# Exp instructions with bias, scale and alpha written as immediates in a four-layer attention kernel

## The chip, the cores and the metric

The kernel runs on one core of one Trainium2 chip. The metric is the device time of one execution in microseconds (us).

Engines in the profile: PE multiplies matrices, PEld loads its weights, ACT is the scalar engine that does the exp, DVE is the vector engine. An ACTIVATE is an instruction of ACT: a function of scale x input + bias. PSUM is the memory that this kernel's matmuls write, SBUF the one where its other tiles are. An operand of an instruction is an immediate when its value stands in the instruction, and a pointer operand when it is read from a tile in SBUF.

## The reference

A 2048x512 activation passes through four layers, each with a layer norm and a residual. Layers 1 and 3 are local dilated attention (window 8). Layers 2 and 4 are full attention with 32 query heads and one shared key and value head of width 16. Those two, cut to what matters:

```python
q = (x @ wq).reshape(B, S, H, Dh).transpose(0, 2, 1, 3)      # S 2048, H 32, Dh 16
k = x @ wk
v = x @ wv
scores = einsum("bhqd,bkd->bhqk", q, k) * Dh ** -0.5
p = softmax(scores)
o = einsum("bhqk,bkd->bhqd", p, v)
return o.transpose(0, 2, 1, 3).reshape(B, S, H * Dh) @ wo
```

Each of the two layers needs 32 x 2048 x 2048 exps.

## The kernel before

A check on the norms of q and k selects a branch that needs no running maximum. There the work is cut into tiles of three chunks, each 128 keys by 512 queries of one head. Per tile: three scores matmuls into PSUM (`st`), one exp over 128x1536 from PSUM to SBUF (`pt`), and three matmuls with the values (`o_ps`). A "block" is 64 chunks. At its end the accumulator is copied and normalized, and four output-projection matmuls (`y`) are queued.

```python
def emit_exp(i):
    cs = chunks[i * tile_chunks:(i + 1) * tile_chunks]
    pt = ptp.tile([128, tile_chunks, 512], BF16, name="pt")
    pt_tiles[i] = pt
    nc.scalar.activation(out=pt[:, :len(cs), :], in_=st_tiles[i][:, :len(cs), :], func=AF.Exp, scale=scale)
    del st_tiles[i]
# ... (emit_scores, finish_block, emit_pv are cut)
for i in range(min(st_bufs, ntiles)):      # st_bufs = 2
    emit_scores(i)
for i in range(ntiles):                    # 683 tiles in each full-attention layer
    cur[0] = i
    emit_exp(i)
    if i + st_bufs < ntiles:
        emit_scores(i + st_bufs)
    emit_pv(i)
    if i % op_every == op_every - 1:       # op_every = 3
        emit_outproj(1, now=i)
```

The argument needs two more instructions, because the kernel carries its own yardstick. Both read a 128x512 fp32 tile from PSUM on ACT. The first has no pointer operand; the second takes its scale from a [128,1] tile:

```python
nc.scalar.activation(out=L[:, w, :], in_=lg[:], func=AF.Identity, scale=scale)                 # line 214
nc.scalar.activation(out=KAB[:, 0, cs], in_=ps[:], func=AF.Identity, scale=kmask[:, 0:1])      # line 354
```

Of the kernel before, what the change touches and what calls it, by code (L numbers as in the profile page):

```python
# [7 lines left out]
F32 = mybir.dt.float32  # L8
AF = mybir.ActivationFunctionType
# [460 lines left out]
def attn_B_fast(ctx, tc, QT, KAB, VE, wo_pad, x_sb, S, tag, tile_chunks=3, st_bufs=2, op_every=3, op_delay=7,  # L470
                on_qc_done=None):
    nc = tc.nc
    NT = S // 128
    NQC = S // 512
    scale = DH ** -0.5
# [16 lines left out]
    st_tiles = {}  # L492
# [14 lines left out]
    def emit_exp(i):  # L507
        cs = chunks[i * tile_chunks:(i + 1) * tile_chunks]
        pt = ptp.tile([128, tile_chunks, 512], BF16, name="pt")
        pt_tiles[i] = pt  # L510
        nc.scalar.activation(out=pt[:, :len(cs), :], in_=st_tiles[i][:, :len(cs), :], func=AF.Exp, scale=scale)  # L511
        del st_tiles[i]

    def emit_outproj(n, now=None):
# [39 lines left out]
    for i in range(ntiles):  # L554
# [5 lines that stand above are left out]
        if i % op_every == op_every - 1:  # L560
            emit_outproj(1, now=i)
# [189 lines left out]
```

## Time and profile before

| | before |
|---|---|
| time, median of the first 3 runs | 2389.79 us (2388.62 to 2390.17) |
| exp, 1366 instructions | 1860.7 us busy, 63.9 us idle before them |
| exp that follows idle, 1536 elements | 1451 ns |
| end to end of back-to-back exps | 1343 ns |
| Identity at 512 elements: no pointer / one pointer | 597 / 687 ns (medians after idle) |

The page: busy time and share of each engine; the chain of waits by line (line 511 is the exp); then the costliest groups: line, engine, operation, output and inputs, count, busy us, mean ns of one, idle us before it and what ended that idle time.

```profile
PE 2085.2 (87%) x11652; PEld 611.5 (26%) x11652; DVE 839.2 (35%) x1061; ACT 2015.7 (84%) x1603; POOL 35.7 (1%) x67
...
ACT pt L511 38%; PE st L503 11%; PE o_ps L547 8%; PE y L520 6%; DVE lb L536 3%; PE ps L184 3%; DVE prod L209 2%; PE y L265 1%; PE ps L359 1%; DVE pv L253 1%; PE acc L256 1%; DVE ot L528 1%; DVE lb L535 1%; DVE onb L537 1%; DVE qsq L373 0%
...
L503 PE MATMUL st<-QT,KAB 32*128 32x512 bf16 x4096 | 859.4, 597 | 176.1 <-ACT pt L511 168.2
L547 PE MATMUL o_ps<-pt,VE 128*32 128x512 bf16 x4096 | 864.7, 607 | 1.4 <-ACT pt L511 1.0
...
L520 PE MATMUL y<-wo_pad,onb 128*128 128x512 bf16 x256 | 155.3, 607 | 20.6 <-DVE onb L537 12.3
```

PE and ACT have similar shares, so the page's first line does not say which of them leads. The window from 300 to 1100 us lies inside the first full-attention layer. This view gives for each engine the busy us (and the instructions), then the granted PE clock:

```profile
core 0: us, PE busy (x) PEld busy (x) DVE busy (x) ACT busy (x) POOL busy (x), PEclk, DMA share, GB/s
300.00:1100.00 800.00, 727.52 (x3535) 174.40 (x3532) 226.03 (x265) 778.64 (x572) 0.00 (x0) 0.50 0.00 1
```

ACT is busy 97% of it (778.64 of 800), PE 91%, at half the clock. The ACT timeline shows the rhythm: start us, length us of the merged run, number of exps at the end of the line, and the idle time before.

```profile
472.74 8.27 ACT L511 ACTIVATE pt<-st 128x1536 bf16<-128x1536 f32 x6 [0.52 <-PE st L503]
481.19 1.45 ACT L511 ACTIVATE pt<-st 128x1536 bf16<-128x1536 f32 x1 [0.18 <-PE st L503]
482.81 25.81 ACT L511 ACTIVATE pt<-st 128x1536 bf16<-128x1536 f32 x19 [0.17 <-PE st L503]
```

Long runs of exps without a gap are tiles in which ACT leads. Lone exps with 0.18 us of idle in front (481.19, then 482.81) are 1.62 us apart: there PE leads, because the four `y` matmuls of a block come in four tiles in a row. The chain of waits shows it in such tiles elsewhere in the layer, with start us, length us and work:

```profile
805.81 0.54 PE y L520
806.35 0.54 PE st L503 x3
806.89 0.54 PE o_ps L547 x3
807.44 0.54 PE y L520
807.98 0.54 PE st L503 x3
808.52 0.55 PE o_ps L547 x3
```

A tile with `y` is three pieces of 0.54 us, 1.63 us in all, which is over the 1.343 us of an exp. Without `y` it would be about 1.08 us (an estimate from the same pieces). The 0.52 us in front of the first run belongs to the end of a block.

From the records, over both layers, I took the 1364 distances from one exp's end to the next. Their median is 1344 ns (1343 within the runs without idle); 144 lie between 1580 and 1680 ns, and 43 are over 1900 ns. In sum they exceed the median by 75 us: 41 us of it in the first set, 29 us in the second.

Groups on ACT with their shapes kept apart:

```profile
L511 ACT ACTIVATE pt<-st 128x1536 bf16<-128x1536 f32 x1364 | 1858.8, 1509 | 63.9 <-PE st L503 62.0
...
L214 ACT ACTIVATE L<-lg 128x512 f32<-128x512 f32 x16 | 9.6, 598 | 70.7 <-PE lg L212 70.7
...
L354 ACT ACTIVATE KAB<-ps,kmask 128x512 bf16<-128x512 f32 x8 | 5.5, 685 | 16.0 <-PE ps L353 16.0
```

Two readings. An operand in a [128,1] tile appears among the inputs (`kmask` on line 354); the exp lists only `st`. And the mean of 1509 ns is not the cost of an exp: back-to-back exps overlap, so a record starts while the one in front still runs. What the span pays is the distance, 1343 ns.

### The profile page before, as it was taken

How to read it: one execution, taken by the hardware profiler on the slowest of the kernel's cores; microseconds unless marked ns; L12 is line 12 of the kernel's file. 1: busy time of each engine (PE TensorE's matmuls, PEld its weight loads, DVE VectorE, ACT ScalarE, POOL GpSimd, SP SyncE). 2: the span in 40 equal slices, each digit the busy share in tenths (PEclk: the TensorE clock that was granted, in tenths of full speed). 3: DMA queues.
4: the chain of work that ended last, by engine and by line, in shares of the span. 5: the costliest groups of instructions: out<-in, count | busy, mean ns of one | idle time of the engine just before them, and what ended most of it. 6: DMA issues, size and time to landing. Idle time of an engine off the chain costs nothing.

```text
span 2389.7 us, 27720 instructions
## 1 busy us (share of the span) xinstructions
PE 2085.2 (87%) x11652; PEld 611.5 (26%) x11652; DVE 839.2 (35%) x1061; ACT 2015.7 (84%) x1603; POOL 35.7 (1%) x67
## 2 busy tenths in 40 slices
PE   5887899999999999999877879999999989999996
PEld 5433222222222222222153332222222222222221
DVE  3875222232223222322339832222222222222222
ACT  5314999999999999999842169999999999999996
POOL 1002000000000000000010000000000000000000
PEclk9998555555555555555589975555555555555555
DMA  1101000000000000000000000000000000000000
GB/s 63 37 2 28 1 1 1 1 1 1 1 1 1 1 1 1 1 1 1 1 3 2 1 1 1 1 1 9 1 1 1 1 10 1 1 9 1 1 1 11
DMA packets 14315, 11.56 MB, mean 5 GB/s; under 512 B 7904, under 2 KB 13536, under 8 KB 14048
## 3 DMA queue, kind: packets, MB, share of 16 engines
q1 hardware_dynamic: 13120, 8.60, 1.4%
q8 instruction: 95, 1.56, 0.3%
q10 hardware_dynamic: 1056, 1.05, 0.1%
q14 instruction: 44, 0.36, 0.1%
HBM read 7.37 MB, written 2.10 MB: 4 GB/s over the span
## 4 chain that ended last, share of the span: by engine, by line
ACT 39%; PE 31%; issue 17%; DVE 12%; POOL 0%; DMA 0%; ACTq 0%; SPq 0%; DVEq 0%; POOLq 0%
ACT pt L511 38%; PE st L503 11%; PE o_ps L547 8%; PE y L520 6%; DVE lb L536 3%; PE ps L184 3%; DVE prod L209 2%; PE y L265 1%; PE ps L359 1%; DVE pv L253 1%; PE acc L256 1%; DVE ot L528 1%; DVE lb L535 1%; DVE onb L537 1%; DVE qsq L373 0%
## 5 line engine op out<-in xcount | busy, mean ns | idle before, releaser
L511 ACT ACTIVATE pt<-st 128x1536 bf16<-128x1536 f32 (+1 forms) x1366 | 1860.7, 1508 | 63.9 <-PE st L503 62.0
L503 PE MATMUL st<-QT,KAB 32*128 32x512 bf16 x4096 | 859.4, 597 | 176.1 <-ACT pt L511 168.2
L547 PE MATMUL o_ps<-pt,VE 128*32 128x512 bf16 x4096 | 864.7, 607 | 1.4 <-ACT pt L511 1.0
L528 DVE COPY ot<-o_ps 128x512 f32<-128x512 f32 x64 | 44.3, 692 | 1163.2 <-PE o_ps L547 1163.2
L503 PEld LDWEIGHTS <-KAB 32*128 32x128 bf16 x4096 | 236.5, 99 | 766.1 <-issue 764.0
L547 PEld LDWEIGHTS <-VE 128*32 128x32 bf16 x4096 | 154.4, 101 | 621.4 <-issue 621.3
L521 DVE TENSOR_TENSOR x_sb<-x_sb,y 128x512 f32<-128x512 f32 x256 | 176.1, 688 | 226.1 <-PE y L520 226.1
L536 DVE RECIPROCAL lb<-lb 128x512 f32<-128x512 f32 (+1 forms) x70 | 214.9, 3075 | 2.1
L520 PE MATMUL y<-wo_pad,onb 128*128 128x512 bf16 x256 | 155.3, 607 | 20.6 <-DVE onb L537 12.3
L89 ACT ACTIVATE xn<-x_sb,ln_nmr,ln_rstd 128x512 bf16<-128x512 f32 x44 | 33.3, 806 | 92.0 <-DVE ln_nmr L83 88.8
L209 DVE TENSOR_TENSOR prod<-Qch,Kch 128x4096 bf16<-128x4096 bf16 x32 | 72.4, 2279 | 58.1 <-ACT Kch L188 56.7
L184 PE MATMUL ps<-xnT,w_sb 128*32 128x512 bf16 x1536 | 90.7, 392 | 1.9 <-ACT Vch L188 1.9
L184 PEld LDWEIGHTS <-w_sb 128*32 128x32 bf16 x1536 | 80.1, 141 | 12.1 <-issue 7.5
L256 PE MATMUL acc<-pv,ident 128*128 128x512 bf16 x256 | 68.7, 402 | 15.9 <-DVE pv L253 10.3
L212 PE MATMUL lg<-prod,ident 128*128 128x512 bf16 x256 | 60.6, 379 | 18.8 <-DVE prod L209 18.8
L258 ACT CAST Och<-acc 128x2048 bf16<-128x2048 f32 x8 | 14.9, 1866 | 72.2 <-PE acc L256 72.2
L253 DVE TENSOR_TENSOR pv<-attn,Vch 128x2048 bf16<-128x2048 bf16 x64 | 73.2, 1222 | 1.5 <-PE acc L256 1.5
L214 ACT ACTIVATE L<-lg 128x512 f32<-128x512 f32 x16 | 9.6, 598 | 70.7 <-PE lg L212 70.7
L99 PE MATMUL pT<-ident,xn 128*128 128x128 bf16 x256 | 27.6, 256 | 44.6 <-ACT xn L89 29.8
L520 PEld LDWEIGHTS <-onb 128*128 128x128 bf16 x256 | 26.4, 103 | 131.6 <-issue 89.7
L535 DVE STREAM_SHUFFLE lb<-ot 128x512 f32<-128x512 f32 (+1 forms) x70 | 46.8, 673 | 0.0
L537 DVE TENSOR_TENSOR onb<-ot,lb 128x512 bf16<-128x512 f32 (+1 forms) x70 | 44.6, 641 | 2.1
(89 smaller groups left out, 538.8 us busy)
## 6 DMA issues: line engine op xcount, KB each, us to landing
xi<-in_A_x_dram SPq DMA_DIRECT2D x4, 512.0 KB, 5.6
wo_r_73<-in_A_wo_dram SPq DMA_DIRECT2D x4, 512.0 KB, 8.2
w_sb<-in_A_wqkv_dram SPq DMA_DIRECT2D x4, 384.0 KB, 8.2
out_dram<-xo SPq DMA_DIRECT2D x2, 512.0 KB, 3.0
out_dram<-xo ACTq DMA_DIRECT2D x2, 512.0 KB, 4.9
wq_sb<-in_B_wq_dram SPq DMA_DIRECT2D x4, 128.0 KB, 3.2
woB_sb<-in_B_wo_dram SPq DMA_DIRECT2D x4, 128.0 KB, 3.7
wo_pad<-in_B_wo_dram SPq DMA_DIRECT2D x16, 32.0 KB, 1.8
```

The costliest lines, as they stand in the source:

```text
L184: nc.tensor.matmul(ps[32 * c:32 * c + 32, :], lhsT=wqkvP[:, kt, j, d, :], rhs=xnT[:, kt, c * 512:(c + 1) * 512], start=(kt == 0), stop=(kt ...
L209: nc.vector.tensor_tensor(out=prod[:], in0=Q[:, dsl, :], in1=K[:, dsl, PAD - DIL * w:PAD - DIL * w + 512], op=ALU.mult)
L253: nc.vector.tensor_tensor(out=pv[:], in0=attn[:, w, :].unsqueeze(1).to_broadcast([PCH, DG, 512]), in1=V[:, ds_, PAD - DIL * w:PAD - DIL * ...
L256: nc.tensor.matmul(acc[:, i, :], lhsT=ident[:PCH, :PCH], rhs=pv[:, i, :], start=(w == 0), stop=(w == W - 1))
L503: nc.tensor.matmul(st[:, n, :], lhsT=KAB[32 * g:32 * g + 32, a, kt * 128:(kt + 1) * 128], rhs=QT[32 * g:32 * g + 32, t, qc * 512:(qc + 1) ...
L511: nc.scalar.activation(out=pt[:, :len(cs), :], in_=st_tiles[i][:, :len(cs), :], func=AF.Exp, scale=scale)
L520: nc.tensor.matmul(y[:], lhsT=onb[:, cols], rhs=wo_pad[:, t, a, :], start=True, stop=True)
L521: nc.vector.tensor_tensor(out=x_sb[:, qt, :], in0=x_sb[:, qt, :], in1=y[:], op=ALU.add)
L535: nc.vector.stream_shuffle(out=lb[:, sl], in_=ot[:, sl], mask=[16] * 32)
L536: nc.vector.reciprocal(out=lb[:, sl], in_=lb[:, sl])
L537: nc.vector.tensor_tensor(out=onb[:, sl], in0=ot[:, sl], in1=lb[:, sl], op=ALU.mult)
L547: nc.tensor.matmul(o_ps[(qc, t, a)][32 * g:32 * g + 32, :], lhsT=VE[:, kt, :], rhs=pt[:, n, :], start=(kt == 0), stop=(kt == NT - 1), tile ...
```

## The change

The intent: an ACTIVATE that takes its bias from a [128,1] tile costs more than one with an immediate. If the default bias of the call were lowered to a pointer to a constant tile, building the instruction by hand with three immediates would take that cost off all 1366 exps.

```diff
-        nc.scalar.activation(out=pt[:, :len(cs), :], in_=st_tiles[i][:, :len(cs), :], func=AF.Exp, scale=scale)
+        ain = nc.scalar.lower_ap(st_tiles[i][:, :len(cs), :])
+        aout = nc.scalar.lower_ap(pt[:, :len(cs), :])
+        imm = lambda v: mybir.ImmediateValue(dtype=F32, value=v)
+        nc.scalar.add_instruction(mybir.InstActivation(name=nc.get_next_instruction_name(), func=AF.Exp,
+            ins=[ain, imm(0.0), imm(scale), imm(0.0)], outs=[aout]))
```

## The prediction

> **What bounds the kernel.** The page gives ACT 84% and PE 87% of the 2389.7 us span. The chain of waits gives 38% to the exp (line 511) and 17% to "issue" (mostly the part of an exp that overlaps its neighbour). The exp group is 1366 instructions, 1860.7 us busy plus 63.9 us idle before them: about 80% of the span. By windows, in 400 to 1150 us ACT is busy 97% and PE about 91%, at a granted clock of 0.50. In order of time, exps of 128x1536 that follow one another without idle end 1343 ns apart. Where ACT leads, the scores matmuls wait for it (168 us over 886 waits). After each block of 64 chunks come several tiles where the output projection makes PE the slower: there exps end 1627 ns apart and wait 0.18 us each.
>
> So 90 ns less per exp, if it shortened the distance, would be worth up to 90 ns x 1366 = 123 us (an estimate), less the PE-paced tiles.
>
> **What the change removes.** By its words, a [128,1] bias pointer on 1366 exps. I do not think it is there. Three signs:
>
> 1. Durations. The Trainium skill, "ScalarE: Activation LUTs", section "What ACT_TABLE_LOAD costs", says each [128,1] pointer operand adds about 93 ns to an ACTIVATE with immediate scale and bias, plus 0.833 ns an element. The trace has the same scale: the logits evacuation (line 214; Identity, scale and bias without a pointer, PSUM, 128x512) takes 597 ns, median; the key copies (line 354; scale from a pointer, same size) 687 ns, so 90 ns for a pointer. An exp that follows idle takes 1451 ns at 1536 elements. From 597 at 512 that is 854 ns for 1024 elements, 0.834 ns each: the exp has exactly the fixed part (about 170 ns) of the pointer-free instruction. With a pointer it should take about 1540.
> 2. The cast evacuations, which have no pointer (586 ns at 512, 1866 at 2048), give the same slope, 0.833.
> 3. The two programs as built, compared instruction by instruction (112,272 of them), are identical except for source line numbers: the exp of the kernel before already carries bias 0.0, scale 0.25 and alpha 0.0 as immediates. The default bias is lowered to an immediate; the edit spells the same instruction by hand.
>
> **What it adds and moves.** Nothing: same waits, same order on each engine, same tiles.
>
> **On the critical path.** 0 us. Prediction: 2389.5 us, range 2385 to 2394 (the three runs before span 1.6 us; another chip may move it by a few us). Faster by over 2%: 1%; within 2%: 98%; slower: 1%.
>
> **What would show each step.** Right: exps after idle still take 1451 ns, back-to-back exps still end 1343 ns apart, 1366 of them busy for about 1861 us; PE waits for ACT about 168 us; every group has the same count and mean within a few ns; the result stays correct and bitwise the same arithmetic. Wrong (a pointer was really removed): the exp after idle drops to about 1360 ns; if in addition the distance falls from 1343 towards 1250 ns, the total falls by up to 5%; if only the duration falls and not the distance, pointer reads were hidden behind the instruction before, and the total stays.
>
> **What would make it wrong.** The kernel that was measured being built differently from the two programs that I compared (another lowering of the default bias); then point 1 would have to be an accident of reading PSUM faster. Or a chip whose clock state differs from that of the runs before.

## More of the kernel before

The kernels of one set of experiments ran in turn on one chip.

In PSUM there are two `st` tiles of 128x1536 fp32, and one tile each of 128x512 for `o_ps` and for `y`.

## The result, and the profile after

Four runs each: 2385.89 us median after (2383.79 to 2390.49), 2389.98 us before (2388.62 to 2392.19). The ratio is 0.9991, 95% interval 0.9974 to 1.0009: the same. The ratios of the experiments below are means of each kernel's runs without its first, profiled one, so they are not quite the ratios of the medians quoted. Executions over 1.5% slower than the fastest of the same kernel are left out of the means. For this first measurement the means of the four runs each give 0.9985, inside the interval too.

The lines of the page and of the ACT groups that answer to those of before (the exp is now line 514, and the lines after it are shifted by 4):

```profile
PE 2054.1 (86%) x11574; PEld 610.7 (26%) x11652; DVE 838.8 (35%) x1061; ACT 2015.1 (84%) x1603; POOL 35.6 (1%) x67
...
L503 PE MATMUL st<-QT,KAB 32*128 32x512 bf16 x4096 | 859.4, 597 | 208.8 <-ACT pt L514 185.7
L551 PE MATMUL o_ps<-pt,VE 128*32 128x512 bf16 x4096 | 864.0, 607 | 1.4 <-ACT pt L514 1.0
...
L524 PE MATMUL y<-wo_pad,onb 128*128 128x512 bf16 x200 | 121.3, 606 | 16.4 <-DVE x_sb L525 15.8
```

```profile
L514 ACT ACTIVATE pt<-st 128x1536 bf16<-128x1536 f32 x1364 | 1858.7, 1513 | 64.6 <-PE st L503 62.3 <-ACT pt L514 0.7
...
L214 ACT ACTIVATE L<-lg 128x512 f32<-128x512 f32 x16 | 9.6, 597 | 70.7 <-PE lg L212 70.7
...
L354 ACT ACTIVATE KAB<-ps,kmask 128x512 bf16<-128x512 f32 x8 | 5.5, 684 | 16.1 <-PE ps L353 16.1
```

And its window and ACT timeline:

```profile
300.00:1100.00 800.00, 715.79 (x3512) 174.13 (x3534) 225.72 (x264) 778.83 (x572) 0.00 (x0) 0.50 0.00 1
```

```profile
473.36 8.27 ACT L514 ACTIVATE pt<-st 128x1536 bf16<-128x1536 f32 x6 [0.52 <-PE st L503]
481.81 1.45 ACT L514 ACTIVATE pt<-st 128x1536 bf16<-128x1536 f32 x1 [0.18 <-PE st L503]
483.43 25.81 ACT L514 ACTIVATE pt<-st 128x1536 bf16<-128x1536 f32 x19 [0.18 <-PE st L503]
```

The timeline is the same to 0.01 us, 0.62 us later. An exp after idle takes 1450 ns (1451 before), back-to-back exps end 1343 ns apart, ACT is busy 778.6 us of the window before and 778.8 us after.

One thing looks like a change and is not. PE is busy 31 us less, and its wait for the exp grew from 168 to 186 us. But PE shows 11,574 matmuls for an unchanged 11,652 weight loads: 78 matmul records are missing, 56 of them `y` (200 in place of 256), and where a record is missing the idle time in front of the next matmul looks longer. Traces below with 11,574 records show it too. The clearest check is o3 and q1 below, which are one and the same kernel on two chips. The trace of o3 has all 11,652 records and that of q1 has 11,574. Their scores groups:

```profile
L505 PE MATMUL st<-QT,KAB 32*128 32x512 bf16 x4096 | 834.2, 598 | 163.7 <-ACT pt L513 158.3
L505 PE MATMUL st<-QT,KAB 32*128 32x512 bf16 x4096 | 834.2, 598 | 189.2 <-ACT pt L513 183.8
```

The same kernel shows 158 us of waits with all records and 184 us with 78 missing. Look at the counts before the busy times.

### The profile page after: what moved, and what is told of

The parts are those of the page before. It is cut to its first block, busy times and chain, and to the rows that moved or that the text cites. A ratio compares the mean times of both kernels' runs of the same rounds, so it can differ in the third digit from the quotient of the medians.

```text
span 2388.7 us, 27642 instructions
## 1 busy us (share of the span) xinstructions
PE 2054.1 (86%) x11574; PEld 610.7 (26%) x11652; DVE 838.8 (35%) x1061; ACT 2015.1 (84%) x1603; POOL 35.6 (1%) x67
## 4 chain that ended last, share of the span: by engine, by line
ACT 37%; PE 32%; issue 17%; DVE 12%; POOL 1%; DMA 0%; SPq 0%; ACTq 0%; DVEq 0%; POOLq 0%
ACT pt L514 36%; PE st L503 11%; PE o_ps L551 10%; PE y L524 4%; DVE lb L540 3%; PE ps L184 3%; DVE prod L209 2%; PE y L265 1%; PE ps L359 1%; DVE pv L253 1%; PE acc L256 1%; DVE ot L532 1%; DVE lb L539 1%; DVE onb L541 1%; DVE ln_stats L79 0%
## 5 line engine op out<-in xcount | busy, mean ns | idle before, releaser
L524 PE MATMUL y<-wo_pad,onb 128*128 128x512 bf16 x200 | 121.3, 606 | 16.4 <-DVE x_sb L525 15.8
```

Source lines behind the costliest of these rows:

```text
L524: nc.tensor.matmul(y[:], lhsT=onb[:, cols], rhs=wo_pad[:, t, a, :], start=True, stop=True)
```

## The experiments

The theory: the two programs are one and the same, since the default bias is already an immediate. Rivals: (R1) the 4 us of the first measurement are a real gain; (R2) a pointer was there and was removed, but its read is hidden behind the exp in front. R2 also asks what a pointer would cost here, so the pointer was put in.

Eleven runs in three sets. All gave correct results except the one that was meant not to.

| run | median us | kernel before, same set | ratio (95%) |
|---|---|---|---|
| n1 the change again | 2389.64 | 2388.20 | 1.0008 (0.9995 to 1.0022) |
| p1 bias pointer | 2470.34 | 2388.20 | 1.0352 (1.0338 to 1.0367) |
| p2 bias and scale pointers | 2574.32 | 2388.20 | 1.0782 (1.0765 to 1.0798) |
| s1 exp over 476 columns | 2293.79 | 2388.20 | 0.9606 (0.9591 to 0.9621) |
| s2 control for s1 | 2388.68 | 2387.91 | 1.0002 (0.9986 to 1.0019) |
| o1 projection spread out | 2341.43 | 2387.91 | 0.9796 (0.9778 to 0.9814) |
| o2 two banks in turn | 2377.56 | 2387.91 | 0.9949 (0.9933 to 0.9966) |
| o3 both | 2311.69 | 2387.91 | 0.9679 (0.9663 to 0.9695) |
| q1 both, again | 2310.98 | 2390.36 | 0.9671 (0.9651 to 0.9690) |
| q2 both, bias pointer | 2430.54 | 2390.36 | 1.0177 (1.0155 to 1.0198) |
| q3 both, exp as in the change | 2311.53 | 2390.36 | 0.9683 (0.9658 to 0.9707) |

### n1: the changed kernel again

No edit.

> The changed kernel once more, with five timed rounds. Theory (both programs are one and the same): ratio 1.000 within 0.2%, exps after idle 1450 ns, back-to-back exps end 1343 ns apart. Rival (the 4 us of the first measurement are real, from something in the edit): ratio 0.998 again, interval clear of 1.

The ratio is 1.0008, and its interval (0.9995 to 1.0022) excludes 0.998: the 4 us did not come back. R1 falls.

### p1 and p2: real pointers

```diff
+    zb = nrm.tile([128, 1], F32, name="zb")
+    nc.vector.memset(zb[:], 0.0)
-        nc.scalar.activation(..., func=AF.Exp, scale=scale)
+        nc.scalar.activation(..., func=AF.Exp, bias=zb[:], scale=scale)
```

p2 has a second such tile, set to the scale and passed as `scale=sb[:]`.

> The exps get a real [128,1] bias pointer to a tile of zeros, so that the pair of this and the kernel before is the change as it was described. Theory A (a pointer's read is hidden behind the exp in front): an exp after idle takes about 1541 ns instead of 1451, back-to-back exps still end 1343 ns apart, total within 0.5% (0 to +12 us). Theory B (each instruction pays it): distance about 1433 ns, total +85 to +115 us (about +4%).

> Bias and scale both from [128,1] pointers. Theory A: after idle about 1631 ns; the distance between back-to-back exps stays 1343 or grows by what no longer fits behind the exp in front; total within 1%. Theory B: distance about 1523 ns, total about +200 us (+8%).

Theory B holds, though p1's total, +82 us, is a little under its range and p2's is +186 us. The exp groups, first of p1, then of p2; the pointer tiles now stand among the inputs, where before and after list only `st`:

```profile
L513 ACT ACTIVATE pt<-st,zb 128x1536 bf16<-128x1536 f32 x1364 | 1966.6, 1582 | 35.5 <-PE st L505 29.6 <-ACT pt L513 0.5
```

```profile
L515 ACT ACTIVATE pt<-st,zb,sb 128x1536 bf16<-128x1536 f32 x1364 | 2081.2, 1728 | 26.8 <-PE st L507 26.5 <-ACT pt L515 0.3
```

| pointers | exp after idle, ns | back-to-back distance, ns | distances of 1580 to 1680 ns |
|---|---|---|---|
| 0 (before) | 1451 | 1343 | 144 |
| 1 (p1) | 1541 | 1431 | 62 |
| 2 (p2) | 1631 | 1522 | 0 |

Each pointer adds 90 ns to the exp and 88 to 91 ns to the distance. At most 2 ns of it are hidden behind the exp in front, so R2 falls too: had a pointer gone, the distance and the total would have shown it. The Trainium skill, "ScalarE: Activation LUTs", section "What ACT_TABLE_LOAD costs", states about 93 ns per pointer operand, and the trace agrees within 5 ns. The page also says that back-to-back ACTIVATEs overlap by about 93 ns, which left open whether the pointer's cost disappears into the overlap. It does not: the duration after idle minus the distance is 108, 110 and 109 ns with none, one and two pointers.

Why +82 us and not 88 x 1366 = 120 us? The timeline of p1 over the part shown of before:

```profile
448.06 30.39 ACT L513 ACTIVATE pt<-st,zb 128x1536 bf16<-128x1536 f32 x21 [0.41 <-PE st L505]
478.83 42.11 ACT L513 ACTIVATE pt<-st,zb 128x1536 bf16<-128x1536 f32 x29 [0.38 <-PE st L505]
```

The lone exps with 0.18 us in front have gone from this stretch; over both layers 62 of the 144 are left, with 0.09 us in front. In those tiles PE led already, so a slower exp first used up its own idle time. In sums: the exp stretches of the two layers grew by 79.5 us; 1364 x 87 ns is 119 us, and the excess over the median distance fell from 75 to 36 us, which takes 39 us off. p2's second pointer found less left to absorb (the excess fell from 36 to 17 us) and added 104 us. One flaw: with the new tile the scheduler also put two matmuls at some block ends the other way round, so p1 and p2 differ from before in that as well. q2 below has no such difference.

### s1 and s2: what 90 ns less would be worth

```diff
+    pt_fix = [ptp.tile([128, tile_chunks, 512], BF16, name=f"ptf{k}", bufs=1) for k in range(3)]
+    for p_ in pt_fix:
+        nc.vector.memset(p_[:], 1.0)
-        pt = ptp.tile([128, tile_chunks, 512], BF16, name="pt")
+        pt = pt_fix[i % 3]
-        nc.scalar.activation(out=pt[:, :len(cs), :], in_=st_tiles[i][:, :len(cs), :], ...)
+        nc.scalar.activation(out=pt[:, :len(cs), :476], in_=st_tiles[i][:, :len(cs), :476], ...)
```

> Wrong result on purpose: each exp covers 476 of its 512 columns, 108 elements or about 90 ns less, with the rest of the pt tiles held at 1.0. It gives what 90 ns per exp would be worth if the change had really taken them from the distance. If the exp sets the pace in most tiles: distance 1253 ns, total -80 to -110 us (-3.5 to -4.5%), the tiles with an output projection still 1627 ns. Rival (PE at the half clock is as slow): distance stays near 1343, total within 1%.

> Control for the 476-column run: the same three fixed pt tiles, all 512 columns. If those tiles cost nothing of themselves: ratio 1.000 within 0.5%, result correct, distance 1343 ns.

s1 gave a wrong result (relative error 0.07). The distance fell to 1253 ns and the total by 94 us; s2 shows that the fixed tiles cost nothing. So the place that the change aimed at was worth having: the exp leads in most tiles, and 90 ns less there would have given 3.9%. The rest of 90 x 1366 = 123 us went to the tiles that PE leads, which did not get shorter: s1 has 190 distances of 1580 to 1680 ns in place of 144, and its excess over the shorter median distance is 104 us in place of 75. The change gave nothing because there was nothing to remove, not because the exp was off the critical path.

### o1, o2, o3: the tiles that PE leads

The source asks for one `y` in three tiles (`op_every = 3`), but in the order as built the scheduler had moved the four together, as the traces show. o1 ties each to the last values matmul issued before it in the source. o2 lets the accumulator and `y` take two PSUM tiles (`bank0` and `bank1`) in turn, so that a new block does not wait for the copy of the old accumulator.

```diff
# o1
-            nc.tensor.matmul(y[:], lhsT=onb[:, cols], rhs=wo_pad[:, t, a, :], start=True, stop=True)
+            i_ = nc.tensor.matmul(y[:], lhsT=onb[:, cols], rhs=wo_pad[:, t, a, :], start=True, stop=True)
+            order_after(tc, i_, last_pv[0])      # last_pv[0]: the last o_ps matmul emitted
# o2
+    banks = [opp.tile([128, 512], F32, name=f"bank{k}") for k in range(2)]
+    block_of = lambda qc, t, a: (qc * 4 + t) * 2 + a
-            y = ypp.tile([128, D], F32, name="y")
+            y = banks[block_of(qt // 4, t, a) % 2]
-                o_ps[(qc, t, a)] = opp.tile([128, 512], F32, name="o_ps")
+                o_ps[(qc, t, a)] = banks[block_of(qc, t, a) % 2]
```

> The four output-projection matmuls of a block are held to one in three tiles instead of four tiles in a row. If they are what makes PE pace those tiles (142 exps that end about 1627 ns apart, 284 ns over 1343): those distances go, total about -40 us (-1.7%). If the pace there is set by something else: no change within 0.5%.

> Two PSUM banks taken in turn by the block's accumulator and by the projection's output, so that the next block does not wait for the copy of the last accumulator. If that wait is the stall at a block's end (about 40 distances of 1960 to 2030 ns, some 650 ns over 1343 each): total about -26 us (-1.1%), fewer than 10 such distances left. Rival: the stall moves to the next wait, total within 0.4%.

> Both order changes, exp as before. If the two stalls add up: nearly all exps 1343 ns apart, total about -66 to -74 us (-2.8 to -3.1%); exp stretch then 1366 x 1343 = 1835 us. Rival: PE at the half clock has too little slack, total -1.5% or less.

o1 took off 46 us: the distances of 1580 to 1680 ns fell from 144 to 1. That shows the cause of those gaps. It fits the lengths above: with one `y` in three tiles PE needs (3 x 1.08 + 0.54) / 3 = 1.26 us a tile (an estimate), less than the 1.343 us of the exp. o2 took off only 10 us, and its expectation (26 us) was half wrong. The distances over 1900 ns did fall, from 43 to 1, and with them 28 us of excess. But those of 1580 to 1680 rose from 144 to 187, which took 12 us back, and other distances took back about 5 us: more than half of the stall moved to other tiles, which was the rival. o3, which does both, takes 76 us off, more than o1 and o2 give singly (57 us) and a little more than expected. In it no distance of either kind is left.

### q1, q2, q3: the same questions where PE leads nowhere

q1 is o3 again. q2 adds the pointer of p1, q3 the spelling of the change. As built, the PE order of the first full-attention layer is identical in all three, and q1's whole program is identical to q3's except for line numbers.

> The version with both order changes once more, as the base for the next run on the same chip: about 0.968 of the kernel before, exps 1343 ns apart nearly throughout.

> The same with a real bias pointer. In the kernel before the pointer cost only about 84 us, less than 88 ns x 1366 = 120 us; if the rest was absorbed by the tiles that PE paced (142 at about 1627 ns), then here, where almost no tile is paced by PE, the pointer should cost nearly all of it: +115 to +122 us over q1. If it was lost elsewhere: about +84 us again.

> The same with the exp spelt as in the changed kernel (explicit immediates). Identical program to q1 as built: ratio to the kernel before equal to q1 within 0.2%. Any 4 us gain of the edit would have to show here too.

The ACT timeline of q1, then of q2, over the stretch shown of before: one unbroken run each (the lines are cut by the window asked for).

```profile
439.50 80.95 ACT L513 ACTIVATE pt<-st 128x1536 bf16<-128x1536 f32 x60
```

```profile
438.52 82.04 ACT L515 ACTIVATE pt<-st,zb 128x1536 bf16<-128x1536 f32 x57
```

In much the same time, 60 exps against 57. The exp groups of q1 and of q2:

```profile
L513 ACT ACTIVATE pt<-st 128x1536 bf16<-128x1536 f32 x1364 | 1833.0, 1652 | 13.3 <-PE st L505 13.1 <-ACT pt L513 0.3
```

```profile
L515 ACT ACTIVATE pt<-st,zb 128x1536 bf16<-128x1536 f32 x1364 | 1953.1, 1865 | 13.1 <-PE st L507 13.1
```

q2 is 119.6 us slower than q1, against 88 x 1366 = 120 us. So the 38 us that p1 did not pay had been absorbed by the tiles that PE led; with none of those, the pointer costs its full price. q3 is within 0.6 us of q1: a second place where the spelling changes nothing. The mean of one exp is 213 ns higher in q2 while the distance grew by 89 ns: in a long run without a gap the starts are closer together than the ends (medians 1330 and 1343 ns in q1, 1424 and 1432 ns in q2), so the records lengthen from one exp to the next. Again the distance is the cost, not the mean.

The kernel of o3 and q1 is the fastest correct version found: 3.3% under the kernel before in q1, with the exp untouched.

## Why the prediction was right

- **Nothing is removed.** Right. It rested on the duration: the casts give a slope of 0.833 ns an element, and the pointer-free 597 ns at 512 elements plus 1024 x 0.833 ns is 1450 ns, against the 1451 ns of the exp. p1 tested that argument: with a pointer the same exp takes 1541 ns, which the prediction had put at about 1540. The comparison of the two built programs said the same without the chip.
- **The total.** Predicted 2389.5 us (2385 to 2394); measured 2385.89, then 2389.64. The 4 us of the first measurement were scatter. That its median still fell in the range was partly luck: two of its four runs (2384.38 and 2383.79) lay below it.
- **The signs in the profile.** The exp after idle, the distance, the exp count and its busy time came out as listed. Two did not: PE's wait for ACT rose from 168 to 186 us, and the `y` group has 200 records in place of 256. Both come from the trace and not from the program, which is the same instruction by instruction: o3 and q1 show the same shift for one kernel.
- **What bounds the kernel.** Right that the exp leads in most tiles and PE in the projection's: s1, o1 and q1 show both halves. The ceiling of 123 us "less the PE-paced tiles" came to 94 us for 90 ns less (s1), 82 us for a pointer more (p1) and 120 us where PE leads nowhere (q2).
- **The hidden read.** The prediction left open that a pointer's read might hide behind the exp in front. It does not.

## What to carry to other kernels

Before writing an instruction by hand to save an operand, look at the operands of the instruction as built, and compare its duration with a sibling in the same trace that is known to have, or to lack, that operand. If an engine leads in a loop, price a saving by the end-to-end distance of its back-to-back instructions, then subtract the iterations that another engine leads. An edit aimed at the right line can still be empty; here the gain at hand was in the order of four small matmuls and in an accumulator that had no second buffer.

## What the Trainium skill lacked or had wrong

- "ScalarE: Activation LUTs", section "What ACT_TABLE_LOAD costs", prices the pointer operand (about 93 ns; here 90 ns on the duration, 88 to 91 ns on the distance) but does not say which form the default bias takes. Here the call without a bias was already an immediate: 1451 ns against 1541 ns with a pointer.
- The same section gives an overlap of about 93 ns for back-to-back ACTIVATEs, without saying whether a pointer's cost falls inside it. Here the overlap, taken as the duration after idle minus the distance, was 108 to 110 ns with none, one or two pointers, and the pointer's cost fell outside.
- The same section gives 186 ns + 0.833 ns an element for an ACTIVATE with immediates. Exps and Identities that read PSUM had the same slope but about 170 ns fixed (1451 at 1536 elements, 597 at 512).
- "TensorE: Matmul & The Clock Gate", Part 1, says that sustained PE activity releases the half-rate clock. In the first full-attention layer the granted clock was 0.50 from 300 to 1100 us while PE was busy 91% of that window; from 100 to 200 us of the same trace it was 0.93 while PE was busy 84%. So in this trace the higher clock does not go with the larger busy share. No run here tells why.
